# The second matrix of layer 1 split into high and low parts on GpSimd when it is converted

## The chip, the cores and the metric

The kernel runs on one core of a Trainium2 chip. The metric is the device time of one execution in microseconds; the kernel before was run three times, and the median is what is compared. TensorE (PE) does the matmuls, ScalarE (ACT) the activations and roundings, VectorE (DVE) and GpSimd (POOL) the elementwise work, and SyncE (SP) issues the transfers between memory and the on-chip buffers. Every engine works through its own list of instructions in order: an instruction that waits holds up all that stand behind it on the same engine.

## The reference

Three parts follow on each other. All inputs are f32 but for the weights of the two layers, which arrive as f64.

```python
scores = np.matmul(q, k.transpose(0, 1, 3, 2)) / np.sqrt(D)     # 4 batches x 8 heads, 576 rows of 64
attn = softmax(where(block_i >= block_j, scores, -1e9))         # blocks of 64 rows
x = np.matmul(attn, v)                                          # as 2304 tokens x 512
h = x @ w_in                                                    # layer 1: 512 -> 2048
x = (h - np.tanh(h)) @ w_out                                    #          2048 -> 512
xn = x / np.sqrt(np.mean(x * x, -1) + 1e-6) * rms_g             # layer 2
out = (silu(xn @ w_gate) * (xn @ w_val)) @ w_out2
```

## The kernel before

The 2304 tokens are worked in six groups of 384. Layer 1 goes over the group's tokens in 16 steps, one for each 128 columns of `w_in` and the 128 rows of `w_out` that belong to them, a chunk each. Attention for the next group's tokens is worked in small pieces between (`aslot`), so that TensorE has a mixture of both; attention for the first group comes ahead of everything, in the front.

A number is carried as two: a high part, rounded to the type fp32r, and a low part, what the rounding left. A product is then three fp32r matmuls (high by high, high by low, low by high). Rounding is `rnd`, on ScalarE an activation with Copy (L103), on another engine a copy that shows up as CAST; the low part is a subtraction, `lo` (L108 for any engine).

A step s of layer 1 has these parts, in this order:
- h, in PSUM: four times three matmuls with the tokens `xh`, `xl` and the chunk's tile of `w_in`, high part in columns 0 to 511, low part in 512 to 1023 (L933 to L935).
- Tanh on ScalarE (L941), then h - tanh h on VectorE.
- For s from 12 (`SPLIT`) on: the result g is split in `gh` (ScalarE, L103) and `gl` (VectorE, L108), and two steps later (`LAG` 2) multiplied by the chunk of `w_out`, three token tiles t by three fp32r matmuls (`gemm_out`, L709 to L711).
- For s below 12, that is in group 0 only: g stays whole in f32 (L945), and one step later it is multiplied by the whole f32 chunk of `w_out`, three f32 matmuls (L719), of which the trace shows two instructions each.

The chunks are converted from f64 in group 0 and the front, in the order `w_in` 0, `w_out` 0, `w_in` 1, and so on (`conv_upto`, `convert1`, `convert`): `stage` loads 512 KB into one of three `st` tiles; ScalarE makes `cv` (a Prelu, L141) and `cu` (a Copy, L143); VectorE bounds `cv` (L144) and merges both (L145, a scalar_tensor_tensor). For a chunk that is split, ScalarE then rounds the high part (L103, `w<-cv`) and VectorE subtracts (L108, `w<-cv,w`); a whole chunk is written by L145 itself. There are two tiles of `cv` and two of `cu`, and `cv` is free for the next but one chunk when the low part has been made.

The converted chunks stand in a ring of four tiles for `w_in` and four for `w_out`. A tile of `w_out` holds one split chunk, or two whole ones, so that up to eight whole chunks are under way. They are stored to memory for the later groups: split ones as `w1d_i` and `w1d_o`, pairs of whole ones as `w1f`. In group 1 the pairs are loaded again (`stagef`, into `st` tiles), split on ScalarE and VectorE (`w1get`, `w<-st`), and stored as `w1d_o`; from then on all chunks come from `w1d_i` and `w1d_o`.

Other names in the rows: `pt` holds the exponentials of attention scores; they are scaled by the sums' reciprocals (`stat`), on GpSimd at L511 for the light head pairs of the front and on ScalarE at L513 later; TensorE transposes them (L526). `kt` and `qt` are copies that GpSimd makes of rows of k and q (L233). L482 are the scores, L578 the products of probabilities and values, `xh` their rounding, `vp` a rounding of values, `x2s` the finished tokens of layer 1 on their way to memory.

The order of TensorE's instructions is that of the program (`manual_schedule`). On the other engines a scheduler sets the order at build time, but for the Prelu, the first Copy and the bounding in `convert`, which keep the order of the program (`pin`).

Of the kernel before, what the change touches and what calls it, by code (L numbers as in the profile page):

```python
# [53 lines left out]
SPLIT = 12  # L54
# [40 lines left out]
def build(ctx, tc, q, k, v, w_in, w_out, w_gate, w_val, w_out2, rms_g, ident_in, out):  # L95
# [18 lines left out]
    w1f = [drm.tile([128, 1024], F32, name=f"w1f_{j}") for j in range(J1 // 2)]  # L114
# [18 lines left out]
    def convert(st, h, l=None):  # L133
# [14 lines left out]
        rnd(ACT, h, f)  # L148
        lo(DVE, l, f, h)
# [443 lines left out]
    with tc.manual_schedule(engines={PE.engine}):  # L593
# [27 lines left out]
        def w1tile(x, last, dt=F32R):  # L621

            n = min(range(4), key=lambda n: lastuse[x][n])
            lastuse[x][n] = last
            return ring.tile([128, 1024], dt, name=f"w1{x}{n}", tag=f"w1{x}{n}")
# [5 lines left out]
        def convert1(n):  # L631
# [8 lines left out]
            if j >= SPLIT:  # L640
                t = wo[j] = w1tile(1, j)
                convert(staged.pop(n), t[:, 0:512], t[:, 512:1024])
                SP.dma_start(out=w1d[1][j], in_=t.bitcast(F32))
                return
            if j % 2 == 0:
                wo["new"] = w1tile(1, j + 1, F32)
            t = wo["new"]
            o = t[:, 512 * (j % 2):512 * (j % 2) + 512]
            convert(staged.pop(n), o)
            wo[j] = o  # L650
            if j % 2:
                SP.dma_start(out=w1f[j // 2], in_=t)

        fstaged = {}

        def stagef(m):
            if m < SPLIT // 2:
                fstaged[m] = env["stg"].tile([128, 1024], F32, name="st", tag="st")
                SP.dma_start(out=fstaged[m], in_=w1f[m])

        def w1get(s):
# [8 lines left out]
            if g == 1 and j < SPLIT:  # L670
                f = fstaged[j // 2][:, 512 * (j % 2):512 * (j % 2) + 512]
                rnd(ACT, t[:, 0:512], f)
                lo(DVE, t[:, 512:1024], f, t[:, 0:512])
                SP.dma_start(out=w1d[1][j], in_=t.bitcast(F32))
                if j % 2:
                    stagef(j // 2 + 3)
            else:
                SP.dma_start(out=t.bitcast(F32), in_=w1d[1][j])
# [5 lines left out]
        def conv_upto(m):  # L684
            nonlocal ncv
            while ncv < min(m, 2 * J1):
                convert1(ncv)
                ncv += 1
                if ncv + 2 < 2 * J1:
                    stage1(ncv + 2)  # L690
                else:
                    stagef(ncv + 2 - 2 * J1)
# [20 lines left out]
        def out1(s, t):  # L713
# [4 lines left out]
            if s < SPLIT:  # L718
# [595 lines left out]
```

## Time and profile before

| | us |
|---|---|
| three runs | 1029.24, 1030.35, 1031.45 |
| median | 1030.35 |
| profiled execution, from the first to the last instruction | 1027.2 |
| TensorE busy | 1008.6 (98%) |
| VectorE busy | 739.5 (72%) |
| ScalarE busy | 663.9 (65%) |
| GpSimd busy | 343.8 (33%) |

The profiled execution's span leaves out what the device time has before the first and behind the last instruction. TensorE's granted clock is 0.999 of its full level over the span. Group 0 goes from about 44 to 137 us. Busy time says how much an engine did, not what it was waited for; that is read from the chain of waits and from what ended an engine's idle time. A duration printed for one instruction can overlap with the next one of the same engine, so for a row of instructions the step from start to start is the better price.

### The profile page before, as it was taken

The page shows a single profiled execution, that of the slowest core. Times are in us where ns is not written, and L with a number is a line of the kernel's source. Part 1 is how long each engine was busy: PE and PEld are TensorE (multiplying, and loading weights), DVE is VectorE, ACT ScalarE, POOL GpSimd, SP SyncE. Part 2 cuts the span into 40 slices and gives each one's busy share as a digit, 9 for nine tenths or more (in the row PEclk, how much of TensorE's full clock was granted, in tenths as well). Part 3 has the DMA queues.
Part 4 walks back from the last instruction along what each step waited for, and adds up shares of the span by engine and source line. Part 5 has one row for each costly group of instructions (what it writes and reads, how often), then busy time and mean ns, then how long its engine had stood idle before and what let it go on. Part 6 is the DMA issues. An engine that isn't in the chain of part 4 may idle for free.

```text
span 1027.2 us, 17940 instructions
## 1 busy us (share of the span) xinstructions
PE 1008.6 (98%) x6026; PEld 930.4 (91%) x6026; DVE 739.5 (72%) x1501; ACT 663.9 (65%) x1529; POOL 343.8 (33%) x467
## 2 busy tenths in 40 slices
PE   7899999999999999999999999999999999999998
PEld 5666788998999999999999989999999999999998
DVE  6977867757777777677657888828866678666775
ACT  6877988768898877688857775615632247412254
POOL 5512112212333153253334425565121480112710
PEclk9999999999999999999999999999999999999999
DMA  9998999897797699667769989985796667876664
GB/s 225 311 341 292 305 324 271 276 234 218 214 251 177 170 285 281 201 226 264 245 214 375 383 322 332 356 334 210 275 340 266 236 230 256 305 275 233 249 229 141
DMA packets 190957, 274.03 MB, mean 267 GB/s; under 512 B 109456, under 2 KB 151184, under 8 KB 184464
## 3 DMA queue, kind: packets, MB, share of 16 engines
q1 hardware_dynamic: 190864, 272.87, 80.9%
q8 instruction: 48, 0.79, 0.3%
q14 instruction: 45, 0.37, 0.1%
HBM read 210.44 MB, written 62.39 MB: 266 GB/s over the span
## 4 chain that ended last, share of the span: by engine, by line
PE 89%; DVE 4%; DMA 3%; ACT 2%; issue 1%; SPq 1%; POOL 0%; DVEq 0%; POOLq 0%
PE t L933 6%; PE t L935 6%; PE t L934 6%; PE t L482 6%; PE gv L1031 5%; PE gv L1029 5%; PE gv L1030 5%; PE acc L709 5%; PE acc L711 5%; PE acc L710 5%; PE t L526 3%; PE ga L1031 3%; PE ga L1029 3%; PE ga L1030 3%; PE acc L719 3%; PE ga L711 2%
## 5 line engine op out<-in xcount | busy, mean ns | idle before, releaser
L933 PE MATMUL t<-xh,w 128*128 128x384 f32 x384 | 137.4, 358 | 0.1
L935 PE MATMUL t<-xh,w 128*128 128x384 f32 x384 | 129.7, 338 | 0.0
L934 PE MATMUL t<-xl,w 128*128 128x384 f32 x384 | 129.3, 337 | 0.0
L709 PE MATMUL acc<-w,gh 128*128 128x512 f32 x252 | 103.3, 410 | 1.0 <-DVE x2s L727 0.8
L1031 PE MATMUL gv<-xh,ws 128*128 128x384 f32 x308 | 103.4, 336 | 0.0
L1030 PE MATMUL gv<-xl,ws 128*128 128x384 f32 x308 | 103.4, 336 | 0.0
L1029 PE MATMUL gv<-xh,ws 128*128 128x384 f32 x308 | 103.3, 336 | 0.0
L711 PE MATMUL acc<-w,gl 128*128 128x512 f32 x252 | 99.6, 395 | 0.3 <-DVE gl L108 0.3
L710 PE MATMUL acc<-w,gh 128*128 128x512 f32 x252 | 99.2, 393 | 0.0
L497 ACT ACTIVATE pt<-pt,stat 128x64 f32<-128x64 f32 (+2 forms) x144 | 80.3, 559 | 26.2 <-DVE pt L495 25.7
L1083 ACT ACTIVATE gt<-c 128x384 f32<-128x384 f32 x29 | 15.2, 525 | 118.8 <-DVE c L1082 118.8
L1086 POOL TENSOR_TENSOR g<-va,vb 128x384 f32<-128x384 f32 x29 | 30.7, 1060 | 154.3 <-ACT va L1085 137.7
L495 DVE TENSOR_SCALAR_CACHE_REDUCE pt<-t 128x64 f32<-128x64 f32 (+2 forms) x144 | 63.8, 449 | 23.1 <-PE t L482 21.8
L933 PEld LDWEIGHTS t<-xh,w 128*128 128x128 f32 x384 | 72.3, 188 | 4.1 <-issue 1.0
L934 PEld LDWEIGHTS t<-xl,w 128*128 128x128 f32 x384 | 72.4, 189 | 2.4
L935 PEld LDWEIGHTS t<-xh,w 128*128 128x128 f32 x384 | 72.0, 188 | 0.0
L108 DVE TENSOR_TENSOR gl<-gt,gh 128x384 fp32r<-128x384 f32 x84 | 55.6, 661 | 18.3 <-ACT gh L103 17.9
L526 PE MATMUL t<-ident,pt 128*128 128x128 f32 x400 | 65.7, 274 | 3.1 <-POOL pt L511 1.6
L108 DVE TENSOR_TENSOR pp<-t,pp 128x512 fp32r<-128x512 f32 (+3 forms) x112 | 55.2, 508 | 15.9 <-ACT pp L103 15.2
L947 DVE TENSOR_TENSOR gt<-t,gt 128x384 f32<-128x384 f32 x84 | 46.2, 550 | 27.6 <-ACT gt L941 27.3
L103 ACT ACTIVATE pp<-t 128x512 fp32r<-128x512 f32 (+5 forms) x144 | 60.7, 436 | 7.7 <-PE t L526 6.9
L526 PEld LDWEIGHTS t<-ident,pt 128*128 128x128 f32 x400 | 50.3, 140 | 15.9 <-POOL pt L511 5.3
(209 smaller groups left out, 3087.7 us busy)
## 6 DMA issues: line engine op xcount, KB each, us to landing
ws<-w2d SPq DMA_DIRECT2D x26, 1792.0 KB, 7.2
w<-w1d_i SPq DMA_DIRECT2D x68, 512.0 KB, 5.1
ws<-wod SPq DMA_DIRECT2D x21, 1536.0 KB, 6.0
w<-w1d_o SPq DMA_DIRECT2D x56, 512.0 KB, 5.1
st<-in_moe_w_out SPq DMA_DIRECT2D x28, 512.0 KB, 5.4
w2d<-wc SPq DMA_DIRECT2D x9, 1024.0 KB, 7.3
st<-in_moe_w_in SPq DMA_DIRECT2D x16, 512.0 KB, 5.8
w1d_i<-w SPq DMA_DIRECT2D x16, 512.0 KB, 5.9
```

The lines of the kernel that those rows point to most:

```text
L108: eng.tensor_tensor(out=o, in0=full, in1=hi.bitcast(F32), op=ALU.subtract)
L497: ACT.activation(out=pt[:, 0:keys], in_=pt[:, 0:keys], func=AF.Exp, scale=-1.0, bias=least, accum_out=st[:, 8 + ti:9 + ti])
L526: PE.transpose(t[:, (j - a) * 128:(j - a + 1) * 128], pt[:, j * 128:(j + 1) * 128], ident)
L709: PE.matmul(acc, lhsT=gh[:, c], rhs=wh, start=first, stop=False, skip_group_check=more)
L710: PE.matmul(acc, lhsT=gh[:, c], rhs=wl, start=False, stop=False, skip_group_check=more)
L711: PE.matmul(acc, lhsT=gl[:, c], rhs=wh, start=False, stop=last, skip_group_check=more)
L933: PE.matmul(h, lhsT=wh[:, c], rhs=xh[:, kk], start=(kk == 0), stop=False)
L934: PE.matmul(h, lhsT=wh[:, c], rhs=xl[:, kk], start=False, stop=False)
L935: PE.matmul(h, lhsT=wl[:, c], rhs=xh[:, kk], start=False, stop=(kk == KD - 1))
L1029: PE.matmul(ps, lhsT=wh[:, c], rhs=xh[:, kk], start=(first and kk == 0), stop=False)
L1030: PE.matmul(ps, lhsT=wh[:, c], rhs=xl[:, kk], start=False, stop=False)
L1031: PE.matmul(ps, lhsT=wl[:, c], rhs=xh[:, kk], start=False, stop=(last and kk == nk - 1))
```

## The change

All 16 chunks of `w_out` are split when they are converted, and both operations of it are put on GpSimd (`convert` has a parameter for the engine; `w_in` stays with ScalarE and VectorE). `SPLIT`, the f32 matmuls, `w1f` and `stagef` are gone. Every step splits g into `gh` and `gl`, the products are always three fp32r matmuls, and the lag is two steps from the start. A tile of `w_out` in the ring always holds one chunk. Stores in group 0 are 16 of `w1d_i` and 16 of `w1d_o`; before they were 16, six of `w1f` and four of `w1d_o`. In group 1 twelve splits with their stores fall away, and twelve loads of `w1d_o` take the place of six of `w1f`.

```diff
-SPLIT = 12
...
-    def convert(st, h, l=None):
+    def convert(st, h, l=None, eng=None):
...
-        rnd(ACT, h, f)
-        lo(DVE, l, f, h)
+        rnd(eng or ACT, h, f)
+        lo(eng or DVE, l, f, h)
...
-            if j >= SPLIT:
-                t = wo[j] = w1tile(1, j)
-                convert(staged.pop(n), t[:, 0:512], t[:, 512:1024])
-                SP.dma_start(out=w1d[1][j], in_=t.bitcast(F32))
-                return
-            if j % 2 == 0:
-                wo["new"] = w1tile(1, j + 1, F32)
-            t = wo["new"]
-            o = t[:, 512 * (j % 2):512 * (j % 2) + 512]
-            convert(staged.pop(n), o)
-            wo[j] = o
-            if j % 2:
-                SP.dma_start(out=w1f[j // 2], in_=t)
...
+            t = wo[j] = w1tile(1, j)
+            convert(staged.pop(n), t[:, 0:512], t[:, 512:1024], POOL)
+            SP.dma_start(out=w1d[1][j], in_=t.bitcast(F32))
...
-            if g == 1 and j < SPLIT:
-                f = fstaged[j // 2][:, 512 * (j % 2):512 * (j % 2) + 512]
-                rnd(ACT, t[:, 0:512], f)
-                lo(DVE, t[:, 512:1024], f, t[:, 0:512])
-                SP.dma_start(out=w1d[1][j], in_=t.bitcast(F32))
-                if j % 2:
-                    stagef(j // 2 + 3)
-            else:
-                SP.dma_start(out=t.bitcast(F32), in_=w1d[1][j])
+            SP.dma_start(out=t.bitcast(F32), in_=w1d[1][j])
...
-            if s < SPLIT:
-                PE.matmul(accs[t], lhsT=gh[:, t * 128:t * 128 + 128], rhs=wo[s], start=(j == 0), stop=(j == J1 - 1))
-            else:
-                gemm_out(accs[t], gh, gl, wo[s][:, 0:512], wo[s][:, 512:1024], t, j == 0, j == J1 - 1)
+            gemm_out(accs[t], gh, gl, wo[s][:, 0:512], wo[s][:, 512:1024], t, j == 0, j == J1 - 1)
...
-            gl = None
-            if s < SPLIT:
-                gh = wk.tile([128, TG], F32, name="gh", tag="gh", bufs=3)
-                DVE.tensor_tensor(gh, h, gt, ALU.subtract)
-            else:
-                DVE.tensor_tensor(gt, h, gt, ALU.subtract)
-                gh = wk.tile([128, TG], F32R, name="gh", tag="gh", bufs=3)
-                gl = wk.tile([128, TG], F32R, name="gl", tag="gl", bufs=3)
-                rnd(ACT, gh, gt)
-                lo(DVE, gl, gt, gh)
+            DVE.tensor_tensor(gt, h, gt, ALU.subtract)
+            gh = wk.tile([128, TG], F32R, name="gh", tag="gh", bufs=3)
+            gl = wk.tile([128, TG], F32R, name="gl", tag="gl", bufs=3)
+            rnd(ACT, gh, gt)
+            lo(DVE, gl, gt, gh)
...
-            if len(pend) > (LAG if s >= SPLIT else 1):
+            if len(pend) > LAG:
```

The scheduler orders the other engines anew. Lines in the changed file are some numbers lower: L139 and L141 make `cv` and `cu` (before L141 and L143), L102, L104 and L107 are rounding on ScalarE, rounding elsewhere and the low part (L103 and L108), L908 is Tanh (L941), L495 the exponential (L497), L509 the scaling (L511), L231 the copies of k and q (L233), and L679 to L681 the fp32r products (L709 to L711).

On TensorE, the end of step 1 and the start of step 2 before: the f32 products of chunk 0 (`w_382`).

```order
L526 MATMUL t<-ident,pt 128x128 x2
L719 MATMUL acc_864<-w_382,gh 128x512
L719 MATMUL acc_866<-w_382,gh 128x512
L719 MATMUL acc_868<-w_382,gh 128x512
L482 MATMUL t<-kh,qf_139 128x384
L933 MATMUL t<-xh,w_580 128x384
```

And after, at the end of step 2:

```order
L524 MATMUL t<-ident,pt 128x128 x3
L679 MATMUL acc_935<-w_374,gh 128x512
L680 MATMUL acc_935<-w_374,gh 128x512
L681 MATMUL acc_935<-w_374,gl 128x512
L524 MATMUL t<-ident,pt 128x128 x3
L679 MATMUL acc_944<-w_374,gh 128x512
L680 MATMUL acc_944<-w_374,gh 128x512
L681 MATMUL acc_944<-w_374,gl 128x512
```

The products of chunk 0 moved from step 1 to step 2 and became three by three matmuls.

On GpSimd, in the front, two triples of scalings before:

```order
L233 COPY kt_603<-kr_479 96x512
L233 COPY qt_605<-qr_481 96x512
L511 TENSOR_SCALAR pt_429<-pt_429,stat_361 128x256
L511 TENSOR_SCALAR pt_429<-pt_429,stat_361 128x320
L511 TENSOR_SCALAR pt_429<-pt_429,stat_361 128x384
L500 MEMSET pt_549 128x64
L511 TENSOR_SCALAR pt_475<-pt_475,stat_474 128x64
```

And after, with the low part of `w_out` 0 (`w110_374`):

```order
L231 COPY kt_601<-kr_474 96x512
L231 COPY qt_603<-qr_476 96x512
L107 TENSOR_TENSOR w110_374<-cv_375,w110_374 128x512
L509 TENSOR_SCALAR pt_424<-pt_424,stat_353 128x256
L509 TENSOR_SCALAR pt_424<-pt_424,stat_353 128x320
L509 TENSOR_SCALAR pt_424<-pt_424,stat_353 128x384
L498 MEMSET pt_547 128x64
L509 TENSOR_SCALAR pt_470<-pt_470,stat_469 128x64
```

The low part stands ahead of a triple of scalings; its CAST stands ahead of the triple before that.

On ScalarE, from the Tanh of step 14 (`gt_1717`) to that of step 15 (`gt_1807`) before; `w111_1645` is the high part of `w_out` 15, and that of `w_in` 15 (`w103_1619`) stands further ahead, between the Tanh of steps 13 and 14.

```order
L103 ACTIVATE w111_1645<-cv_1646 128x512
L941 ACTIVATE gt_1717<-t_1694 128x384
L497 ACTIVATE pt_1732,stat_1731<-pt_1732,stat_1731 128x64
L103 ACTIVATE kh_1752<-t_1747 128x384
L103 ACTIVATE qh0_131<-t_1762 64x6x64
L497 ACTIVATE pt_1732,stat_1731<-pt_1732,stat_1731 128x128
L103 ACTIVATE qh0_131<-t_1762 64x6x64
L103 ACTIVATE gh_1720<-gt_1717 128x384
L103 ACTIVATE w112_1690<-st_1593 128x512
L103 ACTIVATE xh_1001<-t_1786 128x384
L103 ACTIVATE vp_1847<-vr_1460 128x6x64
L941 ACTIVATE gt_1807<-t_1785 128x384
```

And after, from inside step 14 to the Tanh of step 15 (`gt_1931`); `cv_1748` belongs to `w_in` 15, `cv_1772` to `w_out` 15, `w103_1747` is the tile of `w_in` 15:

```order
L102 ACTIVATE qh0_123<-t_1890 64x6x64
L495 ACTIVATE pt_1860,stat_1859<-pt_1860,stat_1859 128x128
L102 ACTIVATE qh0_123<-t_1890 64x6x64
L139 ACTIVATE cv_1748<-st_1630 128x512
L141 ACTIVATE cu_1749<-st_1630 128x512
L102 ACTIVATE xh_1039<-t_1910 128x384
L102 ACTIVATE vp_1969<-vr_1587 128x6x64
L139 ACTIVATE cv_1772<-st_1677 128x512
L141 ACTIVATE cu_1773<-st_1677 128x512
L102 ACTIVATE w103_1747<-cv_1748 128x512
L908 ACTIVATE gt_1931<-t_1909 128x384
```

The two last conversions moved to behind the Tanh of step 14, that of `w_out` 15 behind `xh`, and the high part of `w_in` 15 to the place directly ahead of the Tanh of step 15.

## Rows read from the trace of the kernel before

**Rows 1.** Chain of waits up to 180 us: start, length, what.
```profile
38.99 0.57 ACT cv L141
39.57 0.57 ACT cu L143
...
42.85 0.38 ACT xh L103
...
44.12 0.30 PE t L526
...
122.74 2.58 PE acc L719 x6
```
**Rows 2.** Busy time by stretch: length, each engine (instructions), granted clock, DMA share, GB/s.
```profile
20.00:44.00 24.00, 19.32 (x140) 14.06 (x136) 23.19 (x82) 21.96 (x74) 16.35 (x37) 1.00 1.09 294
44.00:133.00 89.00, 88.88 (x446) 65.35 (x447) 65.80 (x156) 75.16 (x187) 20.67 (x41) 1.00 0.97 319
133.00:180.00 47.00, 46.39 (x271) 42.37 (x272) 33.44 (x89) 37.20 (x104) 7.28 (x14) 1.00 0.94 285
```
**Rows 3.** Timeline of TensorE, chunk 13's products: start, length, engine, line.
```profile
135.06 0.39 PE L709 MATMUL acc<-w,gh 128*128 128x512 f32 x1
...
137.15 0.27 PE L526 MATMUL t<-ident,pt 128*128 128x128 f32 x1
```
**Rows 4.** Instructions by line and shape, ScalarE, 40 to 147: busy, mean ns | idle before.
```profile
L103 ACT ACTIVATE w<-cv 128x512 fp32r<-128x512 f32 x17 | 10.7, 632 | 2.3 <-DVE cv L145 2.2
...
L103 ACT ACTIVATE gh<-gt 128x384 fp32r<-128x384 f32 x5 | 2.6, 529 | 1.0 <-DVE gt L947 1.0
...
L103 ACT ACTIVATE vp<-vr 128x384 fp32r<-128x384 f32 x2 | 1.0, 522 | 0.0
```
**Rows 5.** The same for VectorE.
```profile
L145 DVE SCALAR_TENSOR_TENSOR cv<-cv,cu 128x512 int32<-128x512 int32 x17 | 12.2, 718 | 1.2
...
L108 DVE TENSOR_TENSOR gl<-gt,gh 128x384 fp32r<-128x384 f32 x5 | 2.8, 550 | 0.6 <-ACT gh L103 0.6
```
**Rows 6.** The same for GpSimd, whole span.
```profile
L108 POOL TENSOR_TENSOR kl<-kt,kh 128x576 fp32r<-128x576 f32 x16 | 23.7, 1479 | 32.9 <-ACT kh L103 32.9
...
L108 POOL TENSOR_TENSOR vp<-vr,vp 128x384 fp32r<-128x384 f32 x8 | 8.4, 1049 | 33.0 <-ACT vp L103 25.4 <-DMA kr<-in_k 4.7 <-DMA w1d_i<-w 2.9
...
L233 POOL COPY qt<-qr 96x512 f32<-96x512 f32 x8 | 7.0, 878 | 2.4 <-PE t L246 1.9 <-DMA qr<-in_q 0.5
...
L218 POOL CAST ql<-qf 64x384 fp32r<-64x384 f32 x4 | 2.0, 506 | 0.0
```
**Rows 7.** Timeline of GpSimd in the front; in brackets the idle time before it.
```profile
43.49 2.22 POOL L511 TENSOR_SCALAR pt<-pt,stat 128x256 f32<-128x256 f32 x3 [0.87 <-DVE stat L506]
```
**Rows 8.** Waits of TensorE's weight loads, 20 to 160: total, times, longest.
```profile
PEld t L526 <- POOL pt L511: 4.5, 4, 1.7
...
PEld acc L709 <- DVE x2s L727: 1.0, 1, 1.0
```
**Rows 9.** Timeline of all engines, 113 to 117.
```profile
113.51 1.17 POOL L108 TENSOR_TENSOR vp<-vr,vp 128x384 fp32r<-128x384 f32 x1 [4.67 <-DMA kr<-in_k]
...
113.98 1.25 DVE L108 TENSOR_TENSOR w<-cv,w 128x512 fp32r<-128x512 f32 x1 [0.16 <-ACT w L103]
...
115.89 0.68 DVE L108 TENSOR_TENSOR w<-cv,w 128x512 fp32r<-128x512 f32 x1
```
**Rows 10.** Timeline of all engines, from the end of step 14 to step 15.
```profile
127.74 0.33 PE L935 MATMUL t<-xh,w 128*128 128x384 f32 x1
...
129.55 0.50 ACT L941 ACTIVATE gt<-t 128x384 f32<-128x384 f32 x1
...
131.42 1.52 PE L578 MATMUL t<-pp,vp 128*64 128x384 f32 x12
...
132.87 0.44 PE L933 MATMUL t<-xh,w 128*128 128x384 f32 x1
...
133.10 0.49 ACT L103 ACTIVATE xh<-t 128x384 fp32r<-128x384 f32 x1
```

More of the change, by code (lines that the diff above doesn't have):

```diff
@@ L113, in build @@
     x2d = drm.tile([NT, DM], F32, name="x2d")
-    w1f = [drm.tile([128, 1024], F32, name=f"w1f_{j}") for j in range(J1 // 2)]
     w2d = [drm.tile([128, 2, 7, 256], F32, name=f"w2d_{j}") for j in range(J2)]
@@ L619, in back, with w1tile @@
             return g > 2 and g % 2 == 1
-        def w1tile(x, last, dt=F32R):
+        def w1tile(x, last):
             n = min(range(4), key=lambda n: lastuse[x][n])
             lastuse[x][n] = last
-            return ring.tile([128, 1024], dt, name=f"w1{x}{n}", tag=f"w1{x}{n}")
+            return ring.tile([128, 1024], F32R, name=f"w1{x}{n}", tag=f"w1{x}{n}")
         def until(s):
@@ L639, in convert1 @@
                 return
-            if j >= SPLIT:
-                t = wo[j] = w1tile(1, j)
-                convert(staged.pop(n), t[:, 0:512], t[:, 512:1024])
-                SP.dma_start(out=w1d[1][j], in_=t.bitcast(F32))
-                return
-            if j % 2 == 0:
-                wo["new"] = w1tile(1, j + 1, F32)
-            t = wo["new"]
-            o = t[:, 512 * (j % 2):512 * (j % 2) + 512]
-            convert(staged.pop(n), o)
-            wo[j] = o
-            if j % 2:
-                SP.dma_start(out=w1f[j // 2], in_=t)
[L654 to L659, printed above, removed]
+            t = wo[j] = w1tile(1, j)
+            convert(staged.pop(n), t[:, 0:512], t[:, 512:1024], POOL)
+            SP.dma_start(out=w1d[1][j], in_=t.bitcast(F32))
         def w1get(s):
@@ L688, in conv_upto @@
                 ncv += 1
-                if ncv + 2 < 2 * J1:
-                    stage1(ncv + 2)
-                else:
-                    stagef(ncv + 2 - 2 * J1)
+                stage1(ncv + 2)
         while att.pos < att.end[0]:
@@ L941, in build @@
             ACT.activation(out=gt, in_=h, func=AF.Tanh)
-            gl = None
-            if s < SPLIT:
-                gh = wk.tile([128, TG], F32, name="gh", tag="gh", bufs=3)
-                DVE.tensor_tensor(gh, h, gt, ALU.subtract)
-            else:
-                DVE.tensor_tensor(gt, h, gt, ALU.subtract)
-                gh = wk.tile([128, TG], F32R, name="gh", tag="gh", bufs=3)
-                gl = wk.tile([128, TG], F32R, name="gl", tag="gl", bufs=3)
-                rnd(ACT, gh, gt)
-                lo(DVE, gl, gt, gh)
+            DVE.tensor_tensor(gt, h, gt, ALU.subtract)
[3 more added lines that the diff above has]
+            lo(DVE, gl, gt, gh)
             aslot()
```

## Prediction

> **What bounds the kernel now.** I read the stretches first. In group 0, from 44 to 133 us, TensorE works 88.88 of 89 us, and in the next stretch, which leads into group 1, 46.39 of 47; only before 44 us, where the attention front is built up, does it have holes (19.32 of 24), and its granted clock is at the full level throughout [rows 2]. The chain of waits says the same: up to 44 us it runs through ScalarE, VectorE and DMA, the last of them ScalarE's `xh` at 42.85; from the transposes at 44.12 on it lies on TensorE, through the f32 products at 122.74, with hardly a piece of another engine before group 1 begins [rows 1]. So from 44 us on a TensorE microsecond saved is a microsecond of the kernel, but only while TensorE stays the engine that the others wait for. ScalarE is busy 75.16 of those 89 us, VectorE 65.80, GpSimd 20.67 [rows 2]: the first two have little left, GpSimd has much. The second thing to look at is therefore where an in-order engine could make TensorE wait.
>
> **TensorE's saving.** Before, a chunk below 12 costs three f32 matmuls, each two instructions: six in 2.58 us at 122.74 [rows 1]. After, it costs nine fp32r matmuls; the nine of chunk 13 start at 135.06 and the next work at 137.15, so 2.09 us [rows 3]. That is 0.49 us a chunk, and 12 chunks give **-5.9 us**. The order shows all twelve replaced, and the products one step later; a step more of lag costs TensorE nothing while it has other work, only the buffers of `gh` and `gl` live longer (three of each, enough for a lag of two). Group 0's stretch would shrink from 89 to 83.1 us.
>
> **ScalarE and VectorE in group 0.** ScalarE gains twelve `gh` roundings of 0.529 (6.3 us) and loses the high parts of `w_out` 12 to 15, four of 0.632 (2.5 us) [rows 4]: 79 us of work in 83.1. VectorE gains twelve `gl` subtractions of 0.550 (6.6 us) [rows 5] and loses four low parts of about 0.68, which one took at 115.89 [rows 9] (2.7 us): 69.7 in 83.1. The integer work of `convert` stays, and the subtraction that makes g stays with another name. Both still fit, ScalarE barely, so an average does not decide; the order does.
>
> **GpSimd.** It gets 16 roundings and 16 subtractions of 128x512. No such row exists. A CAST of 64x384 took 0.506, by length 0.67 for 512; a COPY of 96x512 took 0.878; a subtraction took 1.049 at 384 columns and 1.479 at 576, 2.24 ns a column, so 1.34 at 512 [rows 6]. One chunk is then 2.0 to 2.2 us, all of them 32 to 35 us, on an engine with 68 of 89 us free. In itself it hides: `w_out`'s parts are read two steps after the `w_in` chunk of the same number. What it blocks is what stands behind it on its queue.
>
> **The front.** There the probabilities are scaled on GpSimd (L511), and the order puts a low part of 1.34 us ahead of the scaling of columns 256 to 384 for two head pairs, and a CAST ahead of others. The scaling that began at 43.49 had been waited for since 0.87 us, that is, GpSimd was idle then [rows 7]; TensorE's weight loads waited for these scalings four times, 4.5 us in all [rows 8]. Where GpSimd's idle time before a scaling (0.87) is shorter than the work put there (1.34), 0.5 us comes through. Bounds: 0, since the chain up to 44 us names other engines, and 2.7 for twice the whole subtraction. A gain is excluded, nothing is taken off this queue. I take one such remainder, **+0.5**, nearest to the row with the 0.87 gap.
>
> **The step from chunk 14 to 15.** This is the decisive place. A ring tile of `w_out` now holds one chunk instead of two, so the high part of chunk c can be written only when the products of chunk c-4 are done, the `cv` buffer stays taken until GpSimd has made the low part, and the conversions run about a step and a half later. At the end of group 0 nothing is left to take this up. In the order before, ScalarE rounded the last `w_in` chunk ahead of the Tanh of step 14. Now between the Tanh of step 14 and that of step 15 stand, in this sequence: `cv` and `cu` of `w_in` 15, `xh`, `vp`, `cv` and `cu` of `w_out` 15, and only then the high part of `w_in` 15, without which the first matmul of step 15 cannot start. `xh` copies the product of probabilities and values (L578), which on TensorE is the very last work before step 15: in the trace it runs from 131.42, and step 15 follows at once at 132.87 [rows 10]. So from TensorE's last matmul on, five ScalarE instructions must pass. From start to start they take, in the chain, 0.38 (`xh`), 0.57 (`cv`) and 0.57 (`cu`) [rows 1]; `vp` (0.522) and the high part (0.632) [rows 4], less the overlap of 0.1 that `xh` shows (0.49 by itself [rows 10]), give 0.43 and 0.54. Sum 2.5 us with TensorE idle. The low part comes later still: VectorE first merges `w_out` 15 (0.718 [rows 5]) once its `cu` is there, from 1.95 to 2.67, then makes the low part (0.68 [rows 9]), which is done at 3.35, while the third matmul wants it at about 2.85; that is 0.5 more. Then the hand-offs from TensorE to ScalarE, to VectorE and back: in the trace `xh` began at 133.10, 0.16 after the end of L578 at 131.42 + 1.52 [rows 10], so 0.5 for three. It comes to **+3.5**. Bounds: 2.5, the five instructions alone, and 5.0: before, the Tanh of step 14 began at 129.55, 1.5 us after the last matmul of that step ended (127.74 + 0.33) [rows 10], because ScalarE was late, and as much lateness as that would come on top of 3.5.
>
> **Steps 13 and 14, and VectorE beside GpSimd.** The high parts of `w_in` 13 and 14 now also stand only one Tanh ahead of their use, but the work of TensorE between (some 3 us of products and scores) covers Tanh, one exponential and the high part (1.6 us). Bounds 0 and 1.5 us. Then VectorE: at 113.51 GpSimd began a subtraction of 1.17 us, at 113.98 VectorE began a low part from two SBUF operands and took 1.25; the next one, alone, took 0.68 at 115.89 [rows 9]. So such a meeting costs VectorE 0.57. Thirty-two new GpSimd instructions can, once each, cost 18 us. VectorE has 83.1 - 69.7 = 13.4 us of room, 23 meetings. Its work on two SBUF operands in group 0 is 16 `gl`, at most 32 merges and 16 low parts, some 43 of 83 us, so about half of the 32 meet one, and those are hidden but for delays that come through somewhere. For both together I take **+0.8**, nearest to the rows with room.
>
> The Trainium skill (SBUF — State Buffer, Who interferes with whom) states that a VectorE instruction with two SBUF inputs and a GpSimd instruction that reads SBUF take the shared port pair as an exclusive lock, and that the second one blocks for the whole instruction; the pair of rows above agrees. By that rule the new work speaks against this change, since every CAST and subtraction reads SBUF; what would come of it is rival C.
>
> **DMA and group 1.** Sixteen stores of 512 KB in group 0 instead of ten are 3.1 MB more, 10 us of transfer at 319 GB/s [rows 2], spread over some 90 us; in group 1 twelve stores less and six loads more. TensorE waits in neither stretch for a weight load. Group 1 loses 12 roundings on ScalarE and 12 subtractions on VectorE, but TensorE waits there for `x2s` only, 1.0 us for its weights [rows 8], and 47 - 46.39 = 0.6 is all that it was idle in that stretch [rows 2]. A lighter DMA could give back between 0 and 0.6; I take **-0.3**. Later groups are unchanged.
>
> **The sum.** The profiled execution spans 1027.2 us, the median of the runs is 1030.35, so 3.15 us lie around the span; I carry the differences over to the median. -5.9 + 0.5 + 3.5 + 0.8 - 0.3 = -1.4: **1029.0 us**, 0.14% faster, which is within the 0.2% (2.06 us) that a measurement of this kernel can tell from no change.
>
> **Rivals.** A is that forecast, with its own range of 1027.6 to 1030.6: the step to 15 between 2.5 and 5.0, and some tenths of the small terms. *B, the gain mostly stays*: the wait at 15 is at its lower bound, nothing comes through in the front or from VectorE, and group 1 gives its 0.6: 1030.35 - 5.9 + 2.5 - 0.6 = 1026.4. For it speaks that TensorE is the bound at 99.9% and that GpSimd has room; against it the low part on VectorE. A full gain (1024.5) would need step 15 not to wait, and the order excludes that. *C, slower*: VectorE becomes the bound of group 0. It decides from 23 meetings at 0.57 us on; with all 32 VectorE has 69.7 + 18.2 = 87.9 us of work in 83.1, and the excess of about 4 falls on TensorE step by step instead of the small 0.8: 1030.35 - 5.9 + 0.5 + 3.5 + 4.8 - 0.3 = 1033.0. For it speaks the pair of rows 9; against it that the second of a pair is as often GpSimd, which has room. *D, GpSimd's queue delays the front* by its upper bound, 2.7 instead of 0.5: 1031.2. For it speak the four waits for L511; against it the chain. That the change might not do what it says is out: the order shows 36 new triples of matmuls and no f32 product.
>
> **Chances.** A 0.46, B 0.24, D 0.14, C 0.16. Below 1028.29 lies B and the lower edge of A (0.10): faster 0.34. Above 1032.41 lies nearly all of C: slower 0.15. The rest, 0.51, is the same. The range from 1026.0 to 1032.5 leaves out the lowest sixth of B (0.04) and most of C (0.13).
>
> **What would show it.** In the profile after: the nine matmuls of a chunk in 2.1 us for all sixteen; TensorE idle for 3 to 4 us in one piece just ahead of step 15, released by VectorE or ScalarE making `w` (A) or for 2.5 (B); VectorE's `gl` and `w` in group 0 near 0.55 and 0.7 (A, B) or above 1 us (C), with many waits of TensorE in group 0; TensorE's transposes at step 0 later than 44.12 and GpSimd's scaling named as the releaser ahead of it (D). I would be wrong if ScalarE, at 79 of 83 us, held TensorE at many steps and not at one, or if TensorE worked through to step 15 without a hole.

## Result and the profile after

The changed kernel takes 1045.01 us (1043.94 to 1045.45), the kernel before 1029.99 in the same rounds: 1.0134 times as long, interval 1.0118 to 1.015. The ratios given here with an interval are the measurement's own; the quotient of two medians can differ from them by some tenths of a per cent (here it is 1.0146). The forecast was 1029.0 with a range up to 1032.5, so it missed by 16 us and on the wrong side. Each trace is one execution, and two traces of kernels with the same front differ by up to 2.2 us ahead of the first L578 (L576 after the change); times from the traces are therefore differences between two points of one trace.

The busy line of the changed kernel's page, to be held against the table of the kernel before:

```profile
PE 1009.9 (97%) x6062; PEld 939.7 (90%) x6062; DVE 750.4 (72%) x1497; ACT 660.0 (63%) x1525; POOL 372.6 (36%) x499
```

Its stretches, columns as in [rows 2], which they answer to:

```profile
20.00:44.00 24.00, 18.37 (x127) 12.86 (x127) 22.41 (x70) 18.16 (x62) 17.24 (x34) 1.00 1.04 301
44.00:133.00 89.00, 81.18 (x450) 67.83 (x449) 76.47 (x160) 72.16 (x186) 43.48 (x68) 0.98 0.90 291
133.00:145.00 12.00, 8.68 (x52) 6.42 (x52) 9.54 (x21) 10.79 (x26) 4.91 (x8) 0.97 1.07 361
```

GpSimd went from 20.67 to 43.48 us in 44 to 133, TensorE from 88.88 to 81.18. VectorE is busy 76.47 instead of 65.80 although group 0 is not yet over. Taking the first matmul of each step as a mark, the 16.3 us by which the spans of the two traces differ (the medians differ by 15.0) lie here:

| from, to | before | after | difference |
|---|---|---|---|
| start to the first L578/L576 | 19.1 | 19.9 | +0.8 |
| from there to step 0 (the front) | 25.3 | 30.5 | +5.1 |
| step 0 to step 16 (group 0) | 93.1 | 100.4 | +7.3, where -5.9 was forecast for TensorE alone |
| steps 18 and 50 | | | +1.6 and +1.7 |

The steps after those take the same time in both, within 0.2 us in all. The saving itself is there: TensorE's timeline, nine matmuls of a chunk that was f32 before, from 108.14 to the next work at 110.30, 2.16 us against the 2.58 of [rows 1] and near the 2.09 of [rows 3].

```profile
108.14 0.48 PE L679 MATMUL acc<-w,gh 128*128 128x512 f32 x1
...
110.30 0.19 PE L480 MATMUL t<-kh,qh 128*128 128x64 f32 x1
```

**Where the front lost.** The chain of waits of the changed kernel: between two pieces of ScalarE stand 2.56 us of "issue", time for which no releaser is known.

```profile
26.01 0.57 ACT cv L139
26.64 2.56 issue
29.46 0.83 ACT pt L495 x4
```

The timeline of all engines at that place shows why:

```profile
26.60 0.61 POOL L231 COPY kt<-kr 96x512 f32<-96x512 f32 x1
26.61 2.67 DVE L142 TENSOR_SCALAR cv<-cv 128x512 f32<-128x512 f32 x1
...
27.15 0.61 POOL L231 COPY qt<-qr 96x512 f32<-96x512 f32 x1
...
27.73 1.27 POOL L107 TENSOR_TENSOR w<-cv,w 128x512 fp32r<-128x512 f32 x1
...
29.20 0.21 DVE L493 TENSOR_SCALAR_CACHE_REDUCE pt<-t 128x64 f32<-128x64 f32 x1
...
29.46 0.35 ACT L495 ACTIVATE pt<-pt,stat 128x64 f32<-128x64 f32 x1 [0.98 <-DVE pt L493]
```

The bounding of `cv`, 0.42 us by itself, lasts 2.67 us: three GpSimd instructions run back to back from 26.60 to 29.00, the third being the new subtraction, and VectorE's instruction ends 0.28 us after the last of them. It counts as busy all this time. Behind it stands the L493 of the next head pair, behind that ScalarE's exponential. In the trace before, the same instruction met nothing (timeline of VectorE):

```profile
25.83 0.42 DVE L144 TENSOR_SCALAR cv<-cv 128x512 f32<-128x512 f32 x1
```

What ScalarE waits for shows the same in one line. Waits of ScalarE in the front, after (20 to 52), then before (20 to 46): total, times, longest.

```profile
ACT pt L495 <- DVE pt L493: 6.2, 7, 1.3
```
```profile
ACT pt L497 <- DVE pt L495: 1.1, 2, 0.9
```

In the kernel before, the front's chain of waits ran over VectorE, too. Two of its pieces, the second its last ahead of TensorE's step 0:

```profile
38.02 0.35 DVE pt L495 x2
...
43.42 0.57 DVE xl L108
```

**Where group 0 lost.** VectorE's instructions by shape from 20 us to the end of group 0, after and then before (the merge has two lines there, since whole chunks were written at once):

```profile
L143 DVE SCALAR_TENSOR_TENSOR cv<-cv,cu 128x512 int32<-128x512 int32 x31 | 27.8, 897 | 2.6
L142 DVE TENSOR_SCALAR cv<-cv 128x512 f32<-128x512 f32 x31 | 21.1, 679 | 6.2 <-ACT cv L139 6.0
```
```profile
L144 DVE TENSOR_SCALAR cv<-cv 128x512 f32<-128x512 f32 x31 | 13.9, 448 | 7.3 <-ACT cv L141 7.0
L145 DVE SCALAR_TENSOR_TENSOR cv<-cv,cu 128x512 int32<-128x512 int32 x19 | 13.8, 726 | 1.3
L145 DVE SCALAR_TENSOR_TENSOR w<-cv,cu 128x512 int32<-128x512 int32 x12 | 8.7, 721 | 0.9 <-ACT cu L143 0.2
```

Merges took 0.897 us on average instead of 0.724, boundings 0.679 instead of 0.448: 12.5 us more on these two lines alone. Those that met GpSimd make it: sorting the changed kernel's merges by what GpSimd ran beside them, 14 beside nothing took 0.690 on average, and 15 beside an instruction that reads SBUF took 1.116, up to 1.661. The delay reaches TensorE mostly through ScalarE: of the 4.3 us that TensorE waited in group 0 ahead of the hole at step 15, 3.6 ended with ScalarE. ScalarE in turn rounds the high part of `w_in` only when the merge is done. This wait of ScalarE from 20 us to the end of group 0, after and then before:

```profile
ACT w L102 <- DVE cv L143: 10.1, 11, 1.7
```
```profile
ACT w L103 <- DVE cv L145: 2.2, 4, 1.2
```

No wait of ScalarE or VectorE in that stretch ended with GpSimd, nor one of the products with `w_out`, so neither a late part of `w_out` nor a held `cv` shows as a cause. TensorE did wait for GpSimd's scalings of `pt`, 2.2 us in the front (1.3 before). The hole ahead of step 15 came as described; timeline of all engines:

```profile
139.85 1.52 PE L576 MATMUL t<-pp,vp 128*64 128x384 f32 x12
...
141.56 0.49 ACT L102 ACTIVATE xh<-t 128x384 fp32r<-128x384 f32 x1
...
143.48 0.62 ACT L102 ACTIVATE w<-cv 128x512 fp32r<-128x512 f32 x1
...
144.15 0.56 PE L900 MATMUL t<-xh,w 128*128 128x384 f32 x1 [2.78 <-ACT w L102]
...
145.29 0.69 PE L902 MATMUL t<-xh,w 128*128 128x384 f32 x1 [0.26 <-DVE w L107]
```

### The profile page after: what moved, and what is told of

Same layout as the page of the kernel before. It is cut to its first block, busy times and chain, and to the rows that moved or that the text cites. A ratio compares the mean times of both kernels' runs of the same rounds, so it can differ in the third digit from the quotient of the medians.

```text
span 1043.5 us, 18020 instructions
## 1 busy us (share of the span) xinstructions
PE 1009.9 (97%) x6062; PEld 939.7 (90%) x6062; DVE 750.4 (72%) x1497; ACT 660.0 (63%) x1525; POOL 372.6 (36%) x499
## 4 chain that ended last, share of the span: by engine, by line
PE 75%; DVE 11%; ACT 7%; issue 3%; DMA 2%; POOL 1%; SPq 0%; DVEq 0%; ACTq 0%
PE gv L993 5%; PE gv L991 5%; PE gv L992 5%; PE t L480 5%; PE t L900 4%; PE t L902 4%; PE t L901 4%; PE acc L679 4%; PE acc L681 4%; PE acc L680 4%; PE ga L991 3%; PE ga L993 3%; PE ga L992 3%; PE t L524 3%; PE ga L681 2%
## 5 line engine op out<-in xcount | busy, mean ns | idle before, releaser
L679 PE MATMUL acc<-w,gh 128*128 128x512 f32 x288 | 119.2, 414 | 4.1 <-DVE x2s L694 3.9
L681 PE MATMUL acc<-w,gl 128*128 128x512 f32 x288 | 113.8, 395 | 0.0
L680 PE MATMUL acc<-w,gh 128*128 128x512 f32 x288 | 113.2, 393 | 0.0
L993 PE MATMUL gv<-xh,ws 128*128 128x384 f32 x308 | 103.4, 336 | 0.0
L992 PE MATMUL gv<-xl,ws 128*128 128x384 f32 x308 | 103.4, 336 | 0.0
L495 ACT ACTIVATE pt<-pt,stat 128x64 f32<-128x64 f32 (+2 forms) x144 | 80.3, 559 | 30.4 <-DVE pt L493 29.6
L493 DVE TENSOR_SCALAR_CACHE_REDUCE pt<-t 128x64 f32<-128x64 f32 (+2 forms) x144 | 63.9, 448 | 20.9 <-PE t L480 19.8
L107 DVE TENSOR_TENSOR gl<-gt,gh 128x384 fp32r<-128x384 f32 x96 | 64.0, 667 | 20.3 <-ACT gh L102 19.8
L909 DVE TENSOR_TENSOR gt<-t,gt 128x384 f32<-128x384 f32 x96 | 52.9, 551 | 31.3 <-ACT gt L908 31.0
L107 DVE TENSOR_TENSOR pp<-t,pp 128x512 fp32r<-128x512 f32 (+3 forms) x112 | 55.4, 509 | 20.6 <-ACT pp L102 20.0
L102 ACT ACTIVATE gh<-gt 128x384 fp32r<-128x384 f32 x96 | 50.0, 521 | 28.6 <-DVE gt L909 27.8
L679 PEld LDWEIGHTS acc<-w,gh 128*128 128x128 f32 x288 | 54.2, 188 | 13.3 <-DVE x2s L694 5.6
```

The costliest lines, as they stand in the source:

```text
L107: eng.tensor_tensor(out=o, in0=full, in1=hi.bitcast(F32), op=ALU.subtract)
L495: ACT.activation(out=pt[:, 0:keys], in_=pt[:, 0:keys], func=AF.Exp, scale=-1.0, bias=least, accum_out=st[:, 8 + ti:9 + ti])
L679: PE.matmul(acc, lhsT=gh[:, c], rhs=wh, start=first, stop=False, skip_group_check=more)
L680: PE.matmul(acc, lhsT=gh[:, c], rhs=wl, start=False, stop=False, skip_group_check=more)
L681: PE.matmul(acc, lhsT=gl[:, c], rhs=wh, start=False, stop=last, skip_group_check=more)
L992: PE.matmul(ps, lhsT=wh[:, c], rhs=xl[:, kk], start=False, stop=False)
```

## Experiments

**Split on ScalarE and VectorE.** The engine alone is undone.

```diff
-            convert(staged.pop(n), t[:, 0:512], t[:, 512:1024], POOL)
+            convert(staged.pop(n), t[:, 0:512], t[:, 512:1024])
```

> The changed kernel with one edit: the parts of w_out are made on ScalarE and VectorE again (GpSimd gets none of the 32 instructions); ring tiles, lag 2 and the fp32r products stay as changed. Theory T (the 14 us come from GpSimd instructions that read SBUF and block VectorE's instructions beside them): step 0 starts again at 44 to 46 us instead of 50.3, VectorE's merges are back at 0.7 us, and what is left is ScalarE's 9 us of more work in group 0; 1028 to 1036 us. Theory U (they come from the later conversions: one chunk for each ring tile, cv held longer, the order around step 15): step 0 still at 49 us or later, 1041 us or more.

Measured: 1032.03 us, 1.0009 of before (0.999 to 1.0028), 13 us below the changed kernel. Front 26.1 us from the first L576 to step 0 (before 25.3, after 30.5), group 0 89.0 us (93.1, 100.4), merges at 0.713. T holds, U falls. Of the 5.9 us forecast from TensorE, 4.1 arrive in group 0, and 5.9 us are lost again at steps 18, 19 and 50 (more on that below).

**GpSimd work added to the kernel before.** For the twelve whole chunks, at the place where the changed kernel has it, without any use:

```diff
         if l is None:
+            if dummy:
+                POOL.tensor_copy(out=u.bitcast(F32R), in_=h)
+                POOL.tensor_tensor(out=u.bitcast(F32R), in0=h, in1=u.bitcast(F32), op=ALU.subtract)
             return
...
-            convert(staged.pop(n), o)
+            convert(staged.pop(n), o, dummy=True)
```

> The kernel before, with 12 times a CAST and a subtraction of 128x512 added on GpSimd, which read the converted whole chunk and write into the cu tile; nothing uses the result. TensorE, ScalarE, VectorE, ring and lag stay as before, only cu is held until GpSimd is through. T: VectorE's instructions on SBUF operands become longer (merges over 0.9 us on average beside GpSimd, single ones 1.5 to 2.7), step 0 starts 3 to 6 us later, 1036 to 1044 us. U: 1030 us, within 1.5.

And the control, which only writes:

```diff
+            if dummy:
+                for _ in range(4):
+                    POOL.memset(u.bitcast(F32), 0.0)
             return
...
```

> As the run before, but GpSimd does four memsets of 128x512 into the cu tile instead (it writes and reads nothing), 48 in all, about the same GpSimd time. T: VectorE's instructions with two SBUF operands keep 0.69 us beside them, and the time is 1030 to 1033 us. If instead the queue of GpSimd is what costs (its scalings stand behind the new work) or the held cu tile, it is as slow as the run before, 1036 to 1044 us.

Measured: 1037.07 us with the reads (1.0065, 1.0049 to 1.0081) and 1033.69 with the writes (1.0023, 1.001 to 1.0037). The time with reads lies in T's range, though the merges averaged 0.778 us over the stretch to the end of group 0, and 0.886 beside reading GpSimd instructions, a little less than expected; that with writes lies 0.7 us above T's range and clear of the other one. The front took 30.5 and 27.8 us, group 0 93.5 and 93.2, hardly more than the 93.1 of before. So in the front the GpSimd work alone costs what the changed kernel lost there, 5.2 us, and memsets of about the same length cost about half of that. This half is not GpSimd's queue as far as the trace shows: TensorE's waits for the scalings were 1.1 us there (1.3 before), and the longest wait for a held `cu` 0.2. But the six boundings of the front averaged 0.708 us with writes against 0.416 before. In group 0 the kernel before hides the added work; that TensorE there has 5.9 us more of its own work, and ScalarE and VectorE have less, fits this but is not shown by a run.

**The first chunks of the front on ScalarE and VectorE.**

```diff
-            convert(staged.pop(n), t[:, 0:512], t[:, 512:1024], POOL)
+            convert(staged.pop(n), t[:, 0:512], t[:, 512:1024], POOL if j >= EARLY // 2 else None)
```

> The changed kernel, but the first three chunks of w_out, converted in the front, are split on ScalarE and VectorE, chunks 3 to 15 on GpSimd. T: step 0 starts near 45 instead of 50.3, group 0 loses the same as in the changed kernel, 1038 to 1041 us. U: 1043 to 1046 us.

Measured: 1037.09 us (1.0051, 1.0023 to 1.0079), 8 below the changed kernel and 1 below T's range. From the first L576 to step 0 it is 25.5 us, so three chunks on GpSimd made all of the 5.1 us in the front. But group 0 became shorter too, 94.2 instead of 100.4, which neither theory had expected. The hole at step 15 shrinks from 2.78 to 0.71 us; why the rest goes is not shown.

**What else was late: step 15 and `x2s`.** The changed kernel with `w_in` 15 loaded and converted ahead of `w_out` 14:

```diff
+        seq = [*range(2 * J1 - 3), 2 * J1 - 2, 2 * J1 - 3, 2 * J1 - 1]
...
-                convert1(ncv)
+                convert1(seq[ncv])
...
-                stage1(ncv + 2)
+                stage1(seq[ncv + 2] if ncv + 2 < 2 * J1 else 2 * J1)
```

> The changed kernel, but w_in 15 is loaded and converted ahead of w_out 14, so that its high part stands ahead of the Tanh of step 14 on ScalarE. All theories agree on the hole of 3 us ahead of step 15: it goes, and with it 2.5 to 4 us (clock and low part included); 1041 to 1042.5 us. If the time stays at 1044 to 1046, what was late there was not the place of this instruction but the conversions as a whole.

Measured: 1044.35 us. The hole is gone; steps 14 and 15 take 0.4 and 0.0 us more than before, instead of 3.25 and 1.90. Of these 4.8 us the time shows 0.7, so the expected 1041 to 1042.5 was missed: among others, step 18 took 3.0 us more than in the changed kernel, the front of that execution 1.4, and step 0 1.2, with TensorE's granted clock at 0.50 from 48 to 54 us (1.00 in the changed kernel). The place of the instruction was the cause of the hole; by itself, moving it did not give the kernel its time back.

Then the kernel that splits on ScalarE and VectorE, with a third tile for `x2s`:

```diff
-    env["x2s"] = lambda g, t: wk.tile([128, DM], F32, name="x2s", tag="x2s")
+    env["x2s"] = lambda g, t: wk.tile([128, DM], F32, name="x2s", tag="cv" if t == 2 else "x2s")
...
-                    env["x2s"] = lambda g, t: evp.tile([128, DM], F32, name="x2s", tag="x2s")
+                    env["x2s"] = lambda g, t: (wk.tile([128, DM], F32, name="x2s", tag="cv") if t == 2 else
+                                               evp.tile([128, DM], F32, name="x2s", tag="x2s"))
```

> The changed kernel with w_out split on ScalarE and VectorE, and the third x2s tile of a group taken from the cv buffers instead of waiting for the first one's store. If the waits at steps 18 and 50 (2.7 and 2.2 us more than in the kernel before when ScalarE and VectorE split) are waits for the buffer, they go and it is 4 to 5 us faster than that kernel: 1027 to 1028 us where it had 1032.0, and 0.3 to 0.4% faster than the kernel before. If they are something else, 1031 to 1033 us.

Measured: 1024.97 us, 0.9933 of before (0.991 to 0.9955), 2 us below the expected range. Step 18 takes 0.88 us less than before, step 50 the same. It was the buffer: the third tile of a group could be written only when the first one's store had landed, and that took longer in all kernels that came from the changed one without this edit (1.6 to 4.6 us more at step 18) than in those that came from the kernel before (0.4 to 1.0 in the two with added GpSimd work). One such wait in the changed kernel, timeline of VectorE at step 50:

```profile
373.08 0.69 DVE L694 TENSOR_TENSOR x2s<-acc,g_bc 128x512 f32<-128x512 f32 x1 [2.28 <-DMA x2d<-x2s]
```

Why the store lands later is open; it does so with either engine. The same edit in the kernel before:

> The kernel before with one edit, the third x2s tile of a group from the cv buffers. If the gain of the kernel that splits on ScalarE and VectorE and has this edit (1025.0 us) is mostly the edit's, this one is at 1026 or below too. I expect only the wait of 0.6 us at step 18 to go: 1029.5 to 1031, not to be told from the kernel before, so that about 5 of the 6 us are the split's own once the store is out of its way.

Measured: 1028.76 us, 0.9965 (0.9943 to 0.9988), a little more than expected; the trace shows 0.88 us of it at step 18 and 0.5 at step 34. So the split's own gain over that kernel is 3 to 4 us, not 5.

**Which part of the GpSimd work blocks.** Only the subtraction there, the high part on ScalarE:

```diff
-        rnd(eng or ACT, h, f)
+        rnd(ACT, h, f)
```

> The changed kernel with the high part on ScalarE and only the subtraction on GpSimd: 16 instructions of 1.3 us there instead of 32 with 1.9 us a chunk. T: about two thirds of the blocking: step 0 at 47 to 49, 1037 to 1042 us. V: the low part is as late as in the changed kernel, the high part is not; group 0 within 2 us of the changed kernel's 100.4.

Measured: 1037.0 us (1.0055, 1.0039 to 1.0072); front 27.7 us, step 0 at 47.3, group 0 92.6, merges 0.803. T holds, at the lower edge of its range. V falls: it let group 0 shrink by 2 us at most, with the low part on GpSimd as in the changed kernel, and group 0 is 8 us shorter. But this takes a CAST off GpSimd and, by the same edit, gives the high part earlier; the run doesn't part the two.

**Reads against writes, where ScalarE and VectorE are full.** The kernel split on ScalarE and VectorE (busy 84.78 and 78.30 us of 44 to 133), with 32 reading GpSimd instructions added, and then with 64 memsets that take GpSimd as long (about 35 us each):

```diff
         lo(eng or DVE, l, f, h)
+        if dummy:
+            POOL.tensor_copy(out=u.bitcast(F32R), in_=f)
+            POOL.tensor_tensor(out=u.bitcast(F32R), in0=f, in1=u.bitcast(F32), op=ALU.subtract)
...
-            convert(staged.pop(n), t[:, 0:512], t[:, 512:1024], POOL)
+            convert(staged.pop(n), t[:, 0:512], t[:, 512:1024], dummy=True)
```

> The changed kernel with w_out split on ScalarE and VectorE, and in addition the same 32 GpSimd instructions (CAST and subtraction of 128x512 that read cv) into the cu tile, where nothing uses them. T (blocking by what GpSimd reads): step 0 3 to 5 us later than without them, and group 0 (step 0 to step 16) 4 to 11 us longer than its 89.0 us; 1036 to 1046 us. V (group 0 loses because the parts are made late on GpSimd and the order is built around that): group 0 stays at 89 to 90 us, only the front loses; 1034 to 1037 us.

> The control of the run that had 32 GpSimd instructions reading cv added (1051.9 us): the same kernel with w_out split on ScalarE and VectorE, but GpSimd does four memsets of 128x512 for each chunk into the cu tile, 64 in all, 35 us of GpSimd time as there, which read nothing. T: the time is that of the kernel with no added GpSimd work (1032.0) plus 2 to 4 us in the front (the memsets held up the scalings there by 2.5): 1033 to 1037 us, and group 0 takes 89 to 91 us. If the held cu tile or GpSimd's queue made that run slow, this one is at 1046 or more as well.

Measured: 1051.94 us with reads (1.02, 1.0159 to 1.0242) and 1038.81 with writes (1.0054, 1.0023 to 1.0085), against 1032.03 with neither; the first lies 6 us above T's range, the second 2 us above its own, and V falls. Group 0 took 103.4, 94.8 and 89.0 us. VectorE's instructions by shape, 20 us to the end of group 0, with reads:

```profile
L143 DVE SCALAR_TENSOR_TENSOR cv<-cv,cu 128x512 int32<-128x512 int32 x31 | 26.7, 860 | 2.4
L107 DVE TENSOR_TENSOR w<-cv,w 128x512 fp32r<-128x512 f32 x31 | 24.2, 787 | 3.0 <-ACT w L102 2.9
L142 DVE TENSOR_SCALAR cv<-cv 128x512 f32<-128x512 f32 x31 | 15.8, 510 | 3.4 <-ACT cv L139 3.2
```

with writes:

```profile
L143 DVE SCALAR_TENSOR_TENSOR cv<-cv,cu 128x512 int32<-128x512 int32 x30 | 21.9, 731 | 2.1
L107 DVE TENSOR_TENSOR w<-cv,w 128x512 fp32r<-128x512 f32 x30 | 20.8, 693 | 1.3 <-ACT w L102 1.2
L142 DVE TENSOR_SCALAR cv<-cv 128x512 f32<-128x512 f32 x31 | 16.6, 536 | 2.2 <-ACT cv L139 1.7
```

with neither:

```profile
L143 DVE SCALAR_TENSOR_TENSOR cv<-cv,cu 128x512 int32<-128x512 int32 x31 | 22.1, 713 | 1.5
L107 DVE TENSOR_TENSOR w<-cv,w 128x512 fp32r<-128x512 f32 x31 | 21.4, 697 | 2.2 <-ACT w L102 1.9
L142 DVE TENSOR_SCALAR cv<-cv 128x512 f32<-128x512 f32 x31 | 14.7, 476 | 1.8 <-ACT cv L139 1.6
```

The averages of the two-operand instructions (first two lines of each) grow beside reads and hardly beside writes; the bounding, with one operand, grows beside both. Single instructions show it more sharply. In the run with writes, 19 merges and low parts met only memsets, and all took 0.67 to 0.69 us, as those that met nothing; every longer one, up to 1.32, met another GpSimd instruction that reads SBUF. Five boundings that met only memsets took 0.530 on average, up to 0.785, against 0.424 beside nothing. In that run's timeline of all engines a bounding, a low part and a merge stand beside memsets:

```profile
95.30 1.11 POOL L150 MEMSET cu<- 128x512 f32 x2 [4.22 <-DVE cv L143]
95.91 0.79 DVE L142 TENSOR_SCALAR cv<-cv 128x512 f32<-128x512 f32 x1
96.47 1.33 POOL L150 MEMSET cu<- 128x512 f32 x2
96.61 0.67 DVE L107 TENSOR_TENSOR w<-cv,w 128x512 fp32r<-128x512 f32 x1
97.21 0.68 DVE L143 SCALAR_TENSOR_TENSOR cv<-cv,cu 128x512 int32<-128x512 int32 x1
```

So the reads block, and are worth 13 us of the time between the two runs. They also hold `cv`, which the memsets do not, but no wait of ScalarE or VectorE up to group 1 ended with GpSimd in either trace. The writes cost 6.8 us too, more than expected. In group 0 their trace loses 2.1 us of that at step 0, where TensorE's granted clock was 0.50 (48 to 52 us), and 3.3 at steps 13 and 14, with a wait of 1.9 us for a high part of `w_in` ahead of step 14; the front took 3.0 us more. How much of this the longer boundings make, and how much the order of the other engines, which is set anew for each kernel, no run parts.

**The two fixes with either engine.** The fastest kernel has both, `x2s` and `w_in` 15:

> The kernel with w_out split on ScalarE and VectorE and the third x2s tile from cv (1025.0 us), with w_in 15 converted ahead of w_out 14 as well. That kernel has 1.5 us of waits at steps 14 and 15; if they are the high and the low part of w_in 15, 1023.5 to 1024.5 us; if it is the load on ScalarE and VectorE as such, 1025 to 1026.

Measured: 1023.89 us, 0.9915 of before (0.9886 to 0.9943), against 1024.97 without the second. The two times overlap in their noise, but in the trace step 15 lost its 0.8 us, so the last low part was a wait there. And the same with the split on GpSimd:

```diff
-            convert(staged.pop(n), t[:, 0:512], t[:, 512:1024])
+            convert(staged.pop(n), t[:, 0:512], t[:, 512:1024], POOL)
```

> The fastest kernel so far (w_out split on ScalarE and VectorE, third x2s tile from cv, w_in 15 ahead of w_out 14; 1023.9 us) with one edit: w_out's two parts on GpSimd again. T: the waits for x2s (3.3 us) and at step 15 (4.8) are out of the way, what is left of the changed kernel's 14 us is GpSimd's: 5 us in the front and 5 to 8 in group 0, so 1034 to 1038 us, 10 us or more above the same kernel without GpSimd. If the three things only hid one another and the engine costs little by itself, 1024 to 1029.

Measured: 1036.82 us, 1.0046 of before (1.0029 to 1.0063), 12.9 us above the other. By the traces 5.8 lie in the front, 5.6 in group 0 (1.4 at step 7, 4.3 at steps 10 and 11), 1.7 at step 20, where TensorE waited 1.4 us for a load of `w1d_o`. So the engine alone is worth nearly as much as the whole loss. The rest adds up: GpSimd's 12.9 and the 8.2 that step 15 and `x2s` were worth in the changed kernel (1045.01 to 1036.82) make 21.1; the kernel with both fixes and the split on ScalarE and VectorE is 6.1 faster than before (1029.99 to 1023.89), which leaves the 15.0 that were lost.

## Why the prediction was wrong

- **TensorE's saving, -5.9: right in size.** Nine matmuls took 2.16 us; from step 2 to step 6, four chunks without a wait, the changed kernel gains 2.0 us, the 0.49 a chunk that was forecast. Split on ScalarE and VectorE, with the two fixes, group 0 is 88.2 us against 93.1, so 4.9 of the 5.9 arrived there.
- **GpSimd's durations, 2.0 to 2.2 a chunk: nearly right.** A CAST took 0.60 and a subtraction 1.27 where nothing stood beside them, 1.9 in all. "In itself it hides" held for the parts, for which no product waited; it did not hold for what their making did to VectorE.
- **The front, +0.5: measured 5.1. The step that failed first.** I priced only what stands behind the new work on GpSimd's queue, and that was near: TensorE's waits for the scalings grew by 0.9 us. What the work does to VectorE I had priced for group 0 alone. But up to 44 us the chain ran over VectorE as well as ScalarE, so that every lengthened VectorE instruction counts there at once; VectorE was busy 23.19 of 24 us in it [rows 2]. I called ScalarE's `xh` the chain's last piece there; it was VectorE's `xl`, 0.57 us from 43.42. The row for the price was at hand: 1.25 against 0.68 [rows 9]. The upper bound of 2.7 left it out as well.
- **VectorE beside GpSimd, +0.8 with step 13: measured 7.6.** That is what the changed kernel takes longer than with the split on ScalarE and VectorE at steps 6 and 7 (2.5 us), 10 and 11 (3.7) and 13 (1.5), the lower clock behind the waits included. It was the pair of instructions that rival C went by, without VectorE being full as C had it (76.47 of 89 us). Its sign showed only in single instructions: `gl` and `w` averaged 0.661 and 0.780 us, single ones took 1.74 and 2.02, and merges and boundings carried most. Its size failed in three places. The price of a meeting was taken as 0.57; when GpSimd runs several instructions back to back it is as long as all of them, 2.25 us at 26.61. The bounding has one operand, so I left it out; it gained 7.2 us over the front and group 0. And I compared VectorE's sum with a room of 13.4 us in the whole group, while the work goes from ScalarE to VectorE and back several times a step: TensorE waits for the late one in its step, however much room is left in another.
- **Step 15, +3.5: right in place and cause, one term missing.** TensorE was idle for 2.78 us for the high part and 0.26 for the low one, 3.04 in all, a little under the 3.5 of the sum. But the time lost was 3.25 us at step 14 and 1.90 at 15, 5.15 against a bound of 5.0: the sum has nothing for the lower clock behind the hole, nor for waits of the kind that cost 1.5 us at these steps with the split on ScalarE and VectorE, too. Of the 5.15, 4.8 went with the order of `w_in` 15.
- **Group 1, -0.3: measured +1.6, and +1.7 at step 50, in a later group that was called unchanged.** The sign was wrong: the third `x2s` waits for a store, and the store landed later, not earlier. The forecast had "a lighter DMA" there; why the store was late stays open.
- **The total.** Against the forecast the traces have 4.6 us more in the front, 6.8 for VectorE beside GpSimd, 1.7 at step 15 and 3.6 in the later groups. The 3.15 us "around the span" are a misreading without effect: span and median are of different executions there, and the changed kernel's traced execution took 1045.25 us with a span of 1043.5.

TensorE's clock adds to the holes. Its granted clock, the column behind the engines, fell behind two of them; stretches of the changed kernel around 112 us, where TensorE had waited 1.2 us, and the one from 146 us, behind the hole at step 15:

```profile
112.00:114.00 2.00, 1.38 (x8) 1.31 (x9) 1.73 (x4) 2.00 (x5) 2.00 (x5) 0.90 0.89 326
114.00:116.00 2.00, 1.84 (x7) 0.93 (x8) 2.00 (x7) 1.44 (x6) 1.39 (x3) 0.50 0.97 358
116.00:118.00 2.00, 2.00 (x13) 1.15 (x10) 2.00 (x2) 1.96 (x6) 1.74 (x2) 0.74 1.03 311
...
146.00:148.00 2.00, 2.00 (x8) 2.00 (x8) 0.00 (x0) 0.00 (x0) 1.05 (x1) 0.56 0.58 118
```

0.50 is the lower level, 1.2 instead of 2.4 GHz. The `h` matmuls of step 11 take 0.32 us from start to start there instead of 0.17, and L576 2.46 instead of 1.52 us. By such differences it makes some 1.5 us at each of the two holes (an estimate), and it does not occur in group 0 of the trace before. It does not follow every hole: behind the front's last holes, 2.6 and 1.3 us, the clock stayed at 1.00 in the changed kernel.

The Trainium skill (SBUF — State Buffer, Who interferes with whom) says of `tensor_scalar` that, when its operands meet certain conditions, it can enter a mode that uses both port pairs and then contends with GpSimd, and of a VectorE instruction with two SBUF inputs that it contends with a GpSimd instruction that reads SBUF, not with one that only writes it. The runs with reads and with writes agree: 0.510 and 0.536 against 0.476 for the bounding, 0.860 and 0.731 against 0.713 for the merge, 0.787 and 0.693 against 0.697 for the low part. The prediction cited the same section, but not what it says of `tensor_scalar`.

## What to carry to other kernels

Before work is moved to an idle GpSimd, look at what VectorE does at the same time: in these traces an instruction with two SBUF operands waited while GpSimd ran instructions that read SBUF, and the bounding, with one operand in SBUF, beside memsets as well; the wait shows up as busy time. Compare one form's duration alone and beside GpSimd, price the difference first in the stretch where VectorE or ScalarE is on the chain, and do not set it against the room that an average leaves. And make the change once with the engine as it was: the saving on TensorE was real, and with the split on ScalarE and VectorE and two waits taken away the kernel was 0.85% faster than before, of which the `x2s` buffer alone gave the kernel before 0.35%.

## What the runs showed of the hardware

- A VectorE instruction beside three GpSimd instructions without a gap lasted until the last of them had ended: 2.67 us for one of 0.42 (26.61 in the changed kernel), and again 2.67 in the kernel with both fixes and GpSimd. This was not always so: a `gl` of the changed kernel at 90.11 (1.74 us) ended ahead of the third of three, a copy that took 0.94 there instead of 0.61.
- The subtraction from h, which takes one operand from PSUM, did not grow: it stayed at 0.55 us.
- Memsets on GpSimd, which read nothing, left merges at 0.731 us (0.713 with no added work) and low parts at 0.693 (0.697), but the bounding grew from 0.476 to 0.536. Merges and low parts that met nothing but memsets took 0.67 to 0.69.
